# Lead-in of a fused lightning-attention and FFN kernel: decay by pow on GpSimd, copies and scalings moved between engines, matmuls on constants

## The chip, the cores and the metric

The kernel runs on one core of one Trainium2 chip. The metric is the device time of one execution in microseconds (us). Every kernel was run with a profile and then timed in rounds that alternate with runs of the kernel before on the same chip. Each run is labelled fast or slow; for a program on one core, slow means over 1.5% above the fastest run of the same kernel. All comparisons below are between fast runs. The engines are named as in the profile: PE (matmul), PEld (its weight loads), DVE (vector), ACT (scalar), POOL (GpSimd), SP (issues most of the transfers). Lnnn is a line of that kernel, so line numbers shift by a few from kernel to kernel.

## The reference, cut to what matters

```python
def _attn_ref(q, k, v, lam):                 # q, k, v: (4, 8, 768, 64); lam: (8,), 0.97 to 0.99
    block = 64
    Dmask = np.where(rel >= 0, lam[:, None, None] ** rel, 0.0)     # rel = i - j
    ...
    for b in range(nb):
        intra = (q_b k_b^T * Dmask) v_b
        inter = (q_b * lam^(pos+1)) kv_state
        out[b] = intra + inter
        kv_state = lam^block * kv_state + (k_b * lam^(block-1-pos))^T v_b

def _moe_ref(x, w_in, w_out):                # x: (3072, 512), w_in: (512, 2048), w_out: (2048, 512)
    h = x @ w_in
    g = h * np.cos(h)
    return g @ w_out
```

All decay can be put on the inputs: with q scaled by lam^pos and v by lam^-pos, the scores only need a 0/1 mask, and the state is a plain running sum. The position is counted from the middle of the sequence, so the powers run from lam^-384 to lam^383. There are 24 blocks of 128 tokens, six for each of the four sequences.

## The kernel before: the parts that the change touches

The decay factors are two tiles of 128 x 48 (48 = 6 blocks x 8 heads). ACT makes them out of Ln and Exp:

```python
nc.sync.dma_start(out=lam_bc, in_=...)                        # lam on all 128 partitions
nc.gpsimd.iota(pos, pattern=[[P, NB]], base=-S // 2, channel_multiplier=1, ...)
...
lnl = consts.tile([P, H], F32)
nc.scalar.activation(lnl, lam_bc, AF.Ln)
expo = consts.tile([P, NB, H], F32)
nc.vector.tensor_mul(expo, pos (broadcast), lnl (broadcast))
q_scale = consts.tile([P, NB, H], F32)
nc.scalar.activation(q_scale, expo, AF.Exp)
v_scale = consts.tile([P, NB, H], F32)
nc.scalar.activation(v_scale, expo, AF.Exp, scale=-1.0)
warm = consts.tile([P, 1], F32)
nc.scalar.activation(warm, halfpi, AF.Sin)                    # loads the table of the FFN's cosine
```

The work of one block of attention, as small tasks. A planner outside the chip simulates them with the durations given and emits every engine's instructions in the planned order; on the chip each engine runs its list strictly in that order. `early` is true for blocks 0 to 3, which the first FFN unit needs:

```python
early = n < TILES[0]                                          # TILES = [4, 2, 4, 4, 4, 4, 2]

def prep_q():                                                 # q_s = q * q_scale, bf16
    eng = nc.vector if early else nc.gpsimd
    eng.tensor_mul(t, live.pop(("q_f", n)), q_scale[:, c, :]...)
def prep_k():                                                 # k_b, bf16: ACT if early, else GpSimd
def prep_v():                                                 # v_pad = v * v_scale, always GpSimd, two halves
    for i in range(2):
        nc.gpsimd.tensor_mul(v_pad[n % NV][:, i::2, ...], src[:, i::2, :], v_scale[:, c, i::2]...)

def transposes():                                             # 4 of q, 4 of k, into one PSUM bank
    t = bank("ps_t", [P, 2, NP, P], BF16)
    ...
def transposes_out():                                         # one copy of both, on DVE
    nc.vector.tensor_copy(t, live.pop(("t", n)))
def transposes_bd():                                          # q_bd: q block-diagonal, two copies on DVE
...
def update_out():                                             # kv_bd: the state out of PSUM, on DVE
    for i in range(2):
        h = slice(i * D, (i + 1) * D)
        nc.vector.tensor_copy(kv_bd[n % NK][h, :, h], kv_ps[h, :, h])
```

After that come, per block, the scores (PE), the masking s_m (DVE), the values (PE) and their copy into xT (ACT). When xT holds four blocks, the FFN's first unit starts: 16 groups of 4 hidden matmuls, cosine on ACT, gating on DVE, then the projection. The two weights of 2 MB each are issued by GpSimd in four quarters each, and the load of block 4 by SP once the third quarter of the second weight has landed:

```python
ORDER = "b0 b1 b2 b3 i0 i1 i2 i3 o0 o1 o2 o3"                 # b = load of a block, i / o = quarter of w_in / w_out
...
deps = [kept[-2]] if at and (names[at - 1][0] == "b") != (which == "b") else []
```

## Time and profile before

| | before |
|---|---|
| median of four fast runs | 237.86 us (237.16 to 238.0) |
| profiled span | 236.8 us |
| copy of the values of blocks 0, 1, 2, 3 into xT starts at | 13.05, 16.39, 21.27, 25.69 |
| first weight issued / first hidden matmul | 17.21 / 26.32 |
| load of block 4 issued / first projection | 39.02 / 42.81 |

The prediction below shows the lines that this rests on. Two more lines of the kernel before are from its timeline; the columns are start in us, length in us, engine, line, operation, output<-inputs, shapes, number of instructions, and in brackets how long the engine sat idle before and what released it:

```profile
5.52 0.69 DVE L234 TENSOR_TENSOR q_s<-q_f,q_scale 128x512 bf16<-128x512 f32 x1 [1.25 <-ACT q_scale L152]
7.47 1.19 POOL L249 TENSOR_TENSOR v_pad<-v_f,v_scale 128x256 bf16<-128x256 f32 x2 [5.40 <-DMA v_f<-in_v_dram]
```

The first q is scaled at 5.52, as soon as ACT has made q_scale. The first v is scaled at 7.47 and waits for its load, not for v_scale: GpSimd is idle for 5.40 us before it.

### The profile page before, as it was taken

To read this page: it belongs to the slowest core of one execution; us is meant where nothing else is said; L and a number is where in the kernel's file an instruction comes from. 1 tells how busy PE (TensorE), PEld (TensorE's weight loads), DVE (VectorE), ACT (ScalarE), POOL (GpSimd) and SP (SyncE) were. 2 spreads that over 40 slices of the span, in tenths; PEclk is the share of its full clock that TensorE was granted. 3 is DMA by queue.
4 is the path that set the end of the run, shared out by engine and by line. 5 is a ranking of instruction groups with operands and counts; after the bars stand their busy time and mean duration, and the time that the engine had idled before them with its cause. 6 is when DMAs were issued, how large, how long until landed. Compare 5 with 4: busy or idle time off the path is not lost.

```text
span 236.8 us, 3931 instructions
## 1 busy us (share of the span) xinstructions
PE 215.4 (91%) x1447; PEld 123.9 (52%) x1472; DVE 152.8 (65%) x285; ACT 103.7 (44%) x171; POOL 68.6 (29%) x105
## 2 busy tenths in 40 slices
PE   0566799899999999999999999999999999999993
PEld 0455344456677655455555555555555545465641
DVE  5699367376999998986855776685674563433210
ACT  5330277312345446454454444435445345544420
POOL 2339100577767626342242333322000000000000
PEclk9996599999999999999999999999999999999998
DMA  6998999999999999993735110110110111111112
GB/s 125 218 189 142 206 193 197 232 221 214 249 231 233 238 226 244 204 247 64 181 77 136 55 44 0 48 44 1 47 44 4 40 47 44 44 47 44 44 44 89
DMA packets 82722, 29.61 MB, mean 125 GB/s; under 512 B 75536, under 2 KB 79632, under 8 KB 82704
## 3 DMA queue, kind: packets, MB, share of 16 engines
q1 hardware_dynamic: 78480, 25.18, 48.7%
q0 software_dynamic: 4224, 4.19, 10.9%
q8 instruction: 11, 0.18, 0.3%
q14 instruction: 7, 0.06, 0.1%
HBM read 27.27 MB, written 6.29 MB: 142 GB/s over the span
## 4 chain that ended last, share of the span: by engine, by line
PE 77%; DVE 16%; ACT 3%; issue 1%; DMA 1%
PE ps_h L362 30%; PE ps_f L400 30%; DVE q_bd L276 5%; PE ps_o L331 4%; PE ps_t L264 4%; PE ps_s L289 3%; DVE qkT L269 3%; DVE s_m L296 3%; DVE g L375 2%; PE ps_f L362 2%; DVE kv_bd L315 2%; PE ps_o L328 2%; PE ps_s L400 1%; DMA lam_bc<-in_lam_dram 1%; DVE q_s L234 1%
## 5 line engine op out<-in xcount | busy, mean ns | idle before, releaser
L369 ACT ACTIVATE cos<-ps_h,halfpi 128x512 f32<-128x512 f32 (+1 forms) x107 | 66.3, 624 | 75.8 <-PE ps_h L362 73.6
L375 DVE TENSOR_TENSOR g<-ps_h,cos 128x512 bf16<-128x512 f32 (+1 forms) x107 | 64.5, 610 | 51.5 <-ACT cos L369 50.3
L362 PE MATMUL ps_h<-xT,w_in_sb 128*128 128x512 bf16 (+1 forms) x413 | 92.8, 350 | 2.3 <-ACT xT L340 0.7
L400 PE MATMUL ps_f<-w_out_sb,g 128*128 128x512 bf16 x358 | 91.1, 379 | 1.4 <-DVE g L375 0.6
L362 PEld LDWEIGHTS <-w_in_sb 128*128 128x128 bf16 x448 | 43.4, 99 | 38.9 <-issue 4.4
L400 PEld LDWEIGHTS <-g 128*128 128x128 bf16 x384 | 36.4, 98 | 34.7 <-issue 1.3
L249 POOL TENSOR_TENSOR v_pad<-v_f,v_scale 128x256 bf16<-128x256 f32 x48 | 28.8, 621 | 55.1 <-PE ps_o L331 38.9
L296 DVE TENSOR_TENSOR s_m<-ps_s,mask 128x512 bf16<-128x512 f32 x48 | 31.3, 683 | 1.7 <-PE ps_s L289 1.4
L234 POOL TENSOR_TENSOR q_s<-q_f,q_scale 128x512 bf16<-128x512 f32 x20 | 20.9, 1046 | 29.3 <-DMA q_f<-in_q_dram 20.1
L340 ACT CAST xT<-ps_o 128x512 bf16<-128x512 f32 x24 | 14.0, 584 | 28.8 <-PE ps_o L331 28.8
L269 DVE COPY qkT<-ps_t 128x1024 bf16<-128x1024 bf16 x24 | 16.5, 689 | 15.0 <-PE ps_t L264 14.9
L331 PE MATMUL ps_o<-s_m,v_pad 128*128 128x128 bf16 x192 | 20.7, 230 | 1.0 <-DVE s_m L296 0.9
L413 ACT COPY o_sb<-ps_f 128x512 f32<-128x512 f32 x23 | 13.5, 586 | 17.5 <-PE ps_f L400 17.5
L276 DVE COPY q_bd<-qkT 64x512 bf16<-64x512 bf16 x48 | 19.8, 413 | 0.7
L289 PE MATMUL ps_s<-q_bd,qkT 128*128 128x256 bf16 x96 | 16.3, 285 | 4.4 <-DVE q_bd L276 4.3
L331 PEld LDWEIGHTS <-v_pad 128*128 128x128 bf16 x192 | 15.8, 103 | 4.6 <-issue 1.5
L315 DVE CAST kv_bd<-ps_kv 64x256 bf16<-64x256 f32 x40 | 16.8, 419 | 1.5 <-PE ps_kv L309 1.0
L264 PE MATMUL ps_t<-ident,q_s 128*128 128x128 bf16 x96 | 9.8, 227 | 6.8 <-DVE q_s L234 6.7
L328 PE MATMUL ps_o<-qkT,kv_bd 128*128 128x128 bf16 x80 | 15.7, 227 | 0.0
L289 PEld LDWEIGHTS <-qkT 128*128 128x128 bf16 x96 | 8.8, 100 | 12.9 <-DVE q_bd L276 7.6
L243 POOL CAST k_b<-k_f 128x512 bf16<-128x512 f32 x20 | 12.3, 615 | 7.1 <-issue 5.6
L264 PEld LDWEIGHTS <-q_s 128*128 128x128 bf16 x96 | 7.2, 101 | 10.3 <-DVE q_s L234 7.3
(35 smaller groups left out, 77.0 us busy)
## 6 DMA issues: line engine op xcount, KB each, us to landing
q_f<-in_q_dram SPq DMA_DIRECT2D x24, 256.0 KB, 4.9
k_f<-in_k_dram SPq DMA_DIRECT2D x24, 256.0 KB, 5.0
v_f<-in_v_dram SPq DMA_DIRECT2D x24, 256.0 KB, 4.7
out_dram<-o_sb SPq DMA_DIRECT2D x24, 256.0 KB, 2.0
w_in_sb<-in_moe_w_in_dram POOLq DMA_DIRECT2D x4, 512.0 KB, 8.4
w_out_sb<-in_moe_w_out_dram POOLq DMA_DIRECT2D x4, 512.0 KB, 14.8
lam_bc<-in_lam_dram SPq DMA_DIRECT2D x1, 4.0 KB, 2.9
```

Source lines behind the costliest of these rows:

```text
L234: eng.tensor_mul(t, live.pop(("q_f", n)), q_scale[:, c, :].unsqueeze(2).to_broadcast([P, H, D]))
L249: nc.gpsimd.tensor_mul(v_pad[n % NV][:, i::2, i * D:(i + 1) * D], src[:, i::2, :], v_scale[:, c, i::2].unsqueeze(2).to_broadcast([P, NP, D]))
L264: nc.tensor.transpose(t[:, i, p, :], src[:, 2 * p:2 * p + 2, :], ident)
L269: nc.vector.tensor_copy(t, live.pop(("t", n)))
L276: nc.vector.tensor_copy(q_bd[n % NQ][h, :, i, :], t[h, 0, :, :])
L289: nc.tensor.matmul(t[:, 2 * i:2 * i + 2, :], lhsT=live["qkT", n][:, 1, p, :], rhs=q_bd[n % NQ][:, p, :, :], start=True, stop=True)
L296: nc.vector.tensor_mul(live["s_m", n][:, 4 * half:4 * half + 4, :], live.pop(("s", n, half)), mask.unsqueeze(1).to_broadcast([P, 4, P]))
L331: nc.tensor.matmul(t[:, p, :], lhsT=v_pad[n % NV][:, 2 * p + i, :], rhs=live["s_m", n][:, 2 * p + i, :], start=(i == 0 and c == 0), stop=( ...
L362: ins = nc.tensor.matmul(t[:, :cols], lhsT=w_in_sb[:, kd, f * P:(f + 1) * P], rhs=live["xT", i][:, kd, :cols], start=(kd == 0), stop=(kd = ...
L369: nc.scalar.activation(c[:, :cols], live["h", i, f][:, :cols], AF.Sin, bias=halfpi)
L375: nc.vector.tensor_mul(live["g", i][:, f, :cols], live.pop(("h", i, f))[:, :cols], live.pop(("c", i, f))[:, :cols])
L400: nc.tensor.matmul(live["f", i, j], lhsT=live["g", i][:, f, j * P:(j + 1) * P], rhs=w_out_sb[:, f, :], start=(f == 0), stop=(f == KF - 1))
```

## The change

The intent is a shorter lead-in. The decay is made by two `pow` instructions on GpSimd, so ACT needs no Ln, no Exp and only one table load. DVE, which is full up to 25 us, gives the q scaling of blocks 1 to 3 to GpSimd and the copies of the state (kv_bd) of the early blocks to ACT. The transposes of q are copied out apart from those of k, so that q_bd can be made sooner. The first weight waits for block 2 and no longer for block 3. Matmuls on a constant fill PE's gaps up to the first hidden matmul, to keep its clock up. The last tile of the output is copied out by DVE and ACT, half each.

```diff
@@ decay
+    warm = consts.tile([P, 1], F32)
+    nc.scalar.activation(warm, halfpi, AF.Sin)
...
-    lnl = consts.tile([P, H], F32)
-    nc.scalar.activation(lnl, lam_bc, AF.Ln)
-    expo = consts.tile([P, NB, H], F32)
-    nc.vector.tensor_mul(expo, pos.unsqueeze(2).to_broadcast([P, NB, H]),
-                         lnl.unsqueeze(1).to_broadcast([P, NB, H]))
+    neg = consts.tile([P, NB], F32)
+    nc.gpsimd.iota(neg, pattern=[[-P, NB]], base=S // 2, channel_multiplier=-1,
+                   allow_small_or_imprecise_dtypes=True)
     q_scale = consts.tile([P, NB, H], F32)
-    nc.scalar.activation(q_scale, expo, AF.Exp)
     v_scale = consts.tile([P, NB, H], F32)
-    nc.scalar.activation(v_scale, expo, AF.Exp, scale=-1.0)
-    warm = consts.tile([P, 1], F32)
-    nc.scalar.activation(warm, halfpi, AF.Sin)
+    for t, e in ((q_scale, pos), (v_scale, neg)):
+        nc.gpsimd.tensor_tensor(out=t, in0=lam_bc.unsqueeze(1).to_broadcast([P, NB, H]),
+                                in1=e.unsqueeze(2).to_broadcast([P, NB, H]), op=ALU.pow)
@@ q scaling
-            eng = nc.vector if early else nc.gpsimd
+            eng = nc.vector if n == 0 else nc.gpsimd
@@ transposes
+        Tq = pl.add("PE", MM(P, 4), [a], lambda: transposes(0), pa(-0.05), get="ps_t")
+        T[n] = pl.add("PE", MM(P, 4), [b, Tq], lambda: transposes(1), pa(0.0))
+        if early:
+            Toq = pl.add("DVE", 0.42, [Tq], lambda: transposes_out(slice(0, 1)), pa(-0.02), get="qkT")
+            To[n] = pl.add("DVE", 0.42, [T[n], Toq], lambda: transposes_out(slice(1, 2)), pa(0.0))
+            first_out = Toq
+        else:
+            To[n] = first_out = pl.add("DVE", 0.7, [T[n]], lambda: transposes_out(slice(0, 2)), pa(0.0), get="qkT")
+        Tq.frees = [To[n]]
+        Tb[n] = pl.add("DVE", 0.6, [first_out, Sc.get((n - NQ, 1))], transposes_bd, pa(-0.01 if early else 0.1))
@@ state copies
+                    if early:
+                        nc.scalar.copy(kv_bd[n % NK][h, :, h], kv_ps[h, :, h])
+                    else:
+                        nc.vector.tensor_copy(kv_bd[n % NK][h, :, h], kv_ps[h, :, h])
@@ last tile
+                parts = [("DVE", "SP", slice(0, DM // 2)), ("ACT", "ACT", slice(DM // 2, DM))]
@@ release of the weights
-        deps = [kept[-2]] if at and (names[at - 1][0] == "b") != (which == "b") else []
+        deps = [kept[-4 if which != "b" else -2]] if at and (names[at - 1][0] == "b") != (which == "b") else []
@@ idle matmuls
+    def keep_awake(us, at, cols):
+        for _ in range(int(us / (cols / (1200.0 if at < 5.0 else 2400.0) + 0.0025))):
+            nc.tensor.matmul(idle_ps[:, :cols], lhsT=ident, rhs=ident[:, :cols], start=True, stop=True)
... (planner bookkeeping for the split tasks left out)
```

## The prediction

> **What bounds the kernel now.** I read the page's forty slices first, then the table of engines by windows, then the timeline of the first 50 us, and last the answers on the waits of the tensor engine and on the tile of the second weight. The slices:
>
> ```profile
> PE   0566799899999999999999999999999999999993
> ...
> DVE  5699367376999998986855776685674563433210
> ...
> PEclk9996599999999999999999999999999999999998
> DMA  6998999999999999993735110110110111111112
> ```
>
> The matrix engine (PE) is full from the fifth slice to the end, so a microsecond is won only where PE starts late or waits: the lead-in. One slice is 5.9 us. The clock dips in slices 4 and 5. DMA dips once, in slice 3, and is then full to about 105 us. The windows (columns: window and its length, then busy us of PE, weight loads, DVE, ACT, POOL, then clock, DMA share, GB/s):
>
> ```profile
> 15.00:20.00 5.00, 2.96 (x38) 2.11 (x35) 4.88 (x10) 1.20 (x2) 3.58 (x6) 0.99 0.66 101
> 20.00:25.00 5.00, 3.66 (x27) 2.73 (x27) 4.70 (x10) 0.59 (x1) 4.79 (x7) 0.50 1.24 207
> 25.00:30.00 5.00, 4.10 (x15) 1.77 (x14) 0.69 (x1) 1.34 (x3) 0.00 (x0) 0.50 1.24 204
> ...
> 100.00:200.00 100.00, 99.04 (x644) 54.09 (x655) 64.81 (x117) 46.64 (x73) 20.98 (x30) 1.00 0.26 68
> ```
>
> Until 25 us DVE is full (4.7 to 4.9 of 5) and sets the pace of the four blocks of attention that the first FFN unit needs; ACT is nearly free. From 100 us PE is 99% busy. The timeline (start, length, instruction) shows the fence posts:
>
> ```profile
> 14.61 1.19 POOL L249 TENSOR_TENSOR v_pad<-v_f,v_scale 128x256 bf16<-128x256 f32 x2 [2.38 <-DMA v_f<-in_v_dram]
> 17.21 1.68 POOL L213 DMA_DIRECT2D w_in_sb<-in_moe_w_in_dram  x2 [1.41 <-DMA k_f<-in_k_dram]
> 18.90 1.40 POOL L249 TENSOR_TENSOR v_pad<-v_f,v_scale 128x256 bf16<-128x256 f32 x2
> ...
> 21.78 3.00 POOL L216 DMA_DIRECT2D w_out_sb<-in_moe_w_out_dram  x4
> ```
> ```profile
> 25.69 0.59 ACT L340 CAST xT<-ps_o 128x512 bf16<-128x512 f32 x1 [3.83 <-PE ps_o L331]
> 26.32 0.59 PE L362 MATMUL ps_h<-xT,w_in_sb 128*128 128x512 bf16 x1 [0.67 <-ACT xT L340]
> ...
> 39.02 0.37 SPq L198 DMA_DIRECT2D q_f<-in_q_dram  x1
> ...
> 42.81 3.61 PE L400 MATMUL ps_f<-w_out_sb,g 128*128 128x512 bf16 x16 [0.64 <-DVE g L375]
> ```
>
> The FFN starts at 26.3, its first projection at 42.8. The tile view of the second weight ends with its time from issue to landing:
>
> ```profile
> DMA to landing us min/median/max: 12.0/14.8/17.4
> ```
>
> Its four issues run from 21.78 to 24.0, so its last quarter lands at 24.0 + 17.4 = 41.4. The projection at 42.8 finds it there with 1.4 us to spare, while its fourth group of four matmuls needs it only at 42.81 + 3 x 0.865 = 45.4. So the weight stream has 4.0 us of slack, and this number decides my prediction.
>
> **What the Trainium skill says.** "TensorE: Matmul & The Clock Gate", Part 1: the array runs at half clock until a window of about 3.4 us was busy, and falls back after an idle one. The trace agrees: 0.50 from about 19.9 to 29.9, matmul spacing 0.43 us at 27 to 29 and 0.216 us after 30. "ScalarE: Activation LUTs", What ACT_TABLE_LOAD costs, gives about 1283 ns for a load; the trace has three of 1.28 us, two of them behind the decay's Ln and Exp. "GPSIMD Engine Reference", section 3, puts elementwise work with two inputs at about twice DVE's time; the trace has q scaling at 1.046 us on GpSimd against 0.69 on DVE (1.5 times). It has no time for pow, nor has the trace. "DMA: Bandwidth & Descriptors", Issuing engines are not separate DMA queues: transfers share the same 16 engines whoever issues them. The trace agrees in so far as weights and block loads both run at 200 to 220 GB/s, never at their sum.
>
> **The change part by part.**
>
> Decay by pow: takes Ln, Exp and two of three table loads off ACT. Now q_scale is ready at 5.5 and ACT copies the first k at 7.04, straight after the last table load. lam lands at 3.7; with a pow of 48 elements at 1 to 2 us (a guess, ten times a multiply) q_scale comes at 4.8 to 5.8, v_scale at 6 to 8. Gain for block 0: under 1 us, none on the path, since blocks 1 to 3 are paced by their loads (v lands at 7.45, 11.05, 14.6: 3.57 us a block).
>
> DVE's work per block now: q_s 0.69, qkT 0.69, q_bd 0.6 to 0.85, s_m 1.28, kv_bd 0.85, sum 4.1 to 4.4, over the 3.57 of the loads; the backlog grows to the 24.86 at which s_m of block 3 ends. Moved away: q_s of blocks 1 to 3 (0.69 + 0.69 + 0.98 = 2.4) and kv_bd (4 x 0.85 = 3.4). Added: the copy in two halves, 2 x 0.42 for 0.69 (estimate: 0.42 is what DVE takes for half a 0.69 us tile in the gating), 4 x 0.15 = 0.6. Net 5.2 us off DVE; 2.6 to 3.3 per block, under the loads. ACT takes k_b 0.62, kv_bd about 0.8, xT 0.59 = 2.0 of 3.57. POOL takes q_s 1.05 and v_pad 1.19 = 2.24 of 3.57. The lead-in becomes load-bound.
>
> Block 3 then: k lands about 16.9; ACT is through with kv_bd of block 2 and has k_b at 17.9; transposes 18.4, second half copy 18.9, scores 19.5, s_m 20.8, values 21.3, xT 22.0. Against 26.3: 4.3 us earlier.
>
> Release of the first weight by block 2: it may go at 14.6 instead of 17.2. But POOL issues in order. By the planner's rule (of two tasks ready at once attention goes first) v_pad of block 2 (14.61 to 15.8) and the new q_s of block 3 (q lands about 15.7; to 16.9) stand ahead. So the issue comes at about 16.95, 0.25 us earlier and not 2.6. First quarter: the smallest time to landing of this tile is 5.5 us, so 22.45. FFN start about 22.5, 3.8 us earlier.
>
> Idle matmuls: PE is warm at 22.5, so the sixteen hidden groups take 16 x 0.865 = 13.8 us, to 36.35; now they take from 26.3 to 42.2, 15.9. That is 2.0 us more, 5.8 in all at this place. With the wait of 0.64 for gating the projection starts at 37.0.
>
> But its fourth group needs the last quarter of the second weight. All eight quarters move with the first: 41.4 - 0.25 = 41.15. The group is ready to run at 37.0 + 2.6 = 39.6 and waits 1.55. It starts at 41.15 where it started at 45.4: lead 4.25. Then PE waits for the evacuation (0.59 and two hand-overs, about 1.0); before, transposes of block 4 filled 0.6 to 0.8 of that gap. Block 4's load moves only by the 0.25 (its SP issue at 39.02 waits for the third quarter), its k is ready at 44.7, so the transposes come after half of the next projection. Lead left: about 3.5. Blocks 6 and 7 have their k ready 3.2 to 3.5 us before PE transposes them now (52.06 against 55.55, 56.37 against 59.55), so this lead just fits; I take off 0.1 for new small waits: 3.4. After 80 us loads run ahead and PE is the bound, so the lead stays.
>
> Tail: the last tile's evacuation by DVE and ACT halves, 0.4 for 0.59, two stores that share the same engines: 0.15. Sum: 3.4 + 0.15 = 3.55; 237.8 - 3.55 = 234.25.
>
> **Rivals.** (a) The whole 5.8 us arrives, 232.0. For it: PE is full after the lead-in. Against: the 41.4 of the weight stream and block 4's load at 39.0. It needs the first weight issued at about 15 or 15.8, which the order on POOL speaks against. (b) pow is slow. GpSimd is in order; two pows of up to 3.4 us each are caught up by block 3 (it has 1.3 us free per block and 3.7 before the first v). At 5 us each the weight would be issued some 3 us late, and all loads with it: gain about zero, 237 to 238; beyond, slower. Nothing in the profile measures pow. (c) GpSimd and DVE hinder each other in the lead-in: q_bd is 0.59 a pair alone and 0.85 beside GpSimd's weight issue at 17.4, q_s 0.98 in place of 0.69. The FFN then starts at 24; 1.5 us of wait for the weight absorbs that, and the total stays near 234.5. (d) Idle matmuls hold real ones up: at half clock they take 0.11 us instead of 0.058 and the planned 60% of a gap becomes 115%. That costs some tenths per block before the clock rises, also absorbed: 234.5. (e) The static order of all later work is planned anew, worth plus or minus 0.8.
>
> **Range and chances.** Most errors of the lead-in are swallowed by the wait for the weight; the upside is capped by it. Centre 234.2, range 232.8 to 235.9. Faster by over 2% means under 233.05: 0.17, mostly rival (a). Slower by over 2% needs a slow pow: 0.03. Within 2%: 0.80.
>
> **What would show it.** Right: DVE in the window of 15 to 20 well under 4.5 us busy; clock 1.0 from about 10 us on; first hidden matmul at 22 to 23; first weight issue within 0.6 us of 17; PE waiting 1 to 2 us at 39 to 41 inside the first projection; SP's load of block 4 at 38.5 to 39; PE ahead by 3 to 4 us at 100 us. Wrong: a weight issue before 16 or after 18, a pow over 3.4 us, no wait in the first projection, or a lead that has shrunk under 2 us by 100 us because DVE, 95% busy from 60 to 100, cannot follow.

## The result, and the profile after

The changed kernel is slower: 246.73 us median of four fast runs (246.13 to 247.31) against 237.86. The ratio is 1.0379, with a 95% interval of 1.0346 to 1.0412. (A ratio here is the mean time of one kernel's fast runs over that of the other's fast runs of the same rounds, so it is not quite the ratio of the two medians.) The profiled span went from 236.8 to 244.4 us.

| | before | after |
|---|---|---|
| xT copies of blocks 0, 1, 2, 3 start at | 13.05, 16.39, 21.27, 25.69 | 23.13, 27.77, 31.84, 35.27 |
| first weight issued | 17.21 | 26.38 |
| first hidden matmul | 26.32 | 35.91 |
| load of block 4 issued | 39.02 | 48.56 |
| first projection | 42.81 | 50.52 |

These are the forty slices of the changed kernel (6.1 us each; busy tenths of each engine, granted clock of PE in tenths, and the share of the transfer engines):

```profile
PE   4065799979999999999999999999999999999993
...
DVE  4051756735799999898668457756847373342310
...
POOL 6999950027776864532340432232000000000000
PEclk9997999999999999999999999999999999999999
DMA  6990499999999999999546201101100111011112
```

POOL reads 9 in slices 2 to 5, while DVE reads 0, 5, 1 and 7. DMA stands still in slice 4: the first four blocks have landed, and the weights have not been asked for. PE is at 0 in the second slice and reads 9 from the sixth (from 30.5 us) on, with one 7 where the first projection begins; in the kernel before it read 9 from the sixth slice of 5.9 us too (with one 8), but had no empty one behind the first. The windows show the same in figures (window and its length, then busy us of PE, weight loads, DVE, ACT and POOL with their instruction counts, granted clock, share of the transfer engines, GB/s):

```profile
5.00:10.00 5.00, 0.00 (x0) 0.00 (x0) 0.00 (x0) 0.62 (x1) 5.00 (x1) 1.00 1.32 223
...
20.00:25.00 5.00, 3.84 (x40) 3.54 (x39) 1.40 (x4) 1.94 (x4) 5.00 (x8) 0.66 0.01 3
...
100.00:200.00 100.00, 100.00 (x671) 55.03 (x669) 68.52 (x125) 47.10 (x73) 23.70 (x34) 1.00 0.36 87
```

From 5 to 10 us one single POOL instruction fills the whole window, and PE and DVE do nothing at all. From 20 to 25 us transfers run at 3 GB/s. From 100 us PE has no gap (99.04 of 100 us before, with some records missing there). So the time was lost in the lead-in and not won back. The timeline names the instruction:

```profile
3.74 8.05 POOL L155 TENSOR_TENSOR q_scale<-lam_bc,pos 128x48 f32<-128x48 f32 x1 [1.55 <-DMA lam_bc<-in_lam_dram]
11.77 8.00 POOL L155 TENSOR_TENSOR v_scale<-lam_bc,neg 128x48 f32<-128x48 f32 x1
19.84 1.19 POOL L249 TENSOR_TENSOR v_pad<-v_f,v_scale 128x256 bf16<-128x256 f32 x2
...
26.38 0.98 POOL L213 DMA_DIRECT2D w_in_sb<-in_moe_w_in_dram  x1
```

One pow of 48 elements per partition takes 8 us. Two of them hold GpSimd until 19.77, and everything in its queue stands behind them: the first v at 19.84 in place of 7.47, the q of blocks 1 to 3, and last the first weight. The line of v_pad has no bracket any more: its input has long been there, and GpSimd comes to it without a pause. The waits of the first 36 us say the same from the other side (who waited for whom: us in total, times, longest):

```profile
DVE q_s L234 <- POOL q_scale L155: 7.6, 1, 7.6
PE ps_kv L315 <- POOL v_pad L249: 4.6, 1, 4.6
```

DVE waits 7.6 us for the first pow, and PE another 4.6 us for the first v behind the second. The fence posts of the prediction now stand here (timeline; the count in the PE line ends with the window asked for):

```profile
35.27 0.59 ACT L349 CAST xT<-ps_o 128x512 bf16<-128x512 f32 x1 [0.23 <-PE ps_o L340]
35.91 1.45 PE L371 MATMUL ps_h<-xT,w_in_sb 128*128 128x512 bf16 x6
...
48.56 0.37 SPq L198 DMA_DIRECT2D q_f<-in_q_dram  x1
```

The hidden matmuls start when the xT copy of block 3 ends (35.27 + 0.59 = 35.86). The first weight quarter was issued at 26.38, and the shortest time to landing of a quarter in this trace is 5.5 us, so it was there at about 32 (an estimate from these two numbers). It is the attention of the first four blocks, not the weight, that set the start.

At the end of the kernel, the split of the last copy can be read off the timelines. Before, and then after:

```profile
232.85 0.59 ACT L413 COPY o_sb<-ps_s 128x512 f32<-128x512 f32 x1 [2.00 <-PE ps_s L400]
```
```profile
240.53 0.42 DVE L422 COPY o_sb<-ps_s 128x256 f32<-128x256 f32 x1 [5.92 <-DMA out_dram<-o_sb]
240.99 0.37 ACT L422 COPY o_sb<-ps_s 128x256 f32<-128x256 f32 x1 [2.46 <-DVE o_sb L422]
```

The halves did not run side by side. ACT's half starts when DVE's is done (240.53 + 0.42 = 240.95) and is shown as released by it, so it waits for a semaphore of DVE's; no run tried it without this wait. From the start of the copy to the end of the span it is 236.8 - 232.85 = 3.95 us before and 244.4 - 240.53 = 3.87 after, so 0.08 us was won.

### The profile page after: what moved, and what is told of

It reads as the page before. It is cut to its first block, busy times and chain, and to the rows that moved or that the text cites. A ratio compares the mean times of both kernels' runs of the same rounds, so it can differ in the third digit from the quotient of the medians.

```text
span 244.4 us, 4231 instructions
## 1 busy us (share of the span) xinstructions
PE 221.6 (91%) x1608; PEld 131.3 (54%) x1608; DVE 147.4 (60%) x278; ACT 103.6 (42%) x174; POOL 88.0 (36%) x111
## 4 chain that ended last, share of the span: by engine, by line
PE 76%; DVE 11%; POOL 5%; issue 3%; DMA 2%; ACT 2%; POOLq 0%
PE ps_f L409 31%; PE ps_h L371 29%; PE ps_o L340 4%; DVE q_bd L276 3%; PE ps_s L295 3%; PE ps_t L265 3%; POOL v_scale L155 3%; DVE g L384 3%; DVE qkT L270 2%; DVE s_m L302 2%; PE ps_f L371 2%; PE ps_kv L315 2%; POOL q_scale L155 1%; PE ps_o L337 1%; DMA lam_bc<-in_lam_dram 1%
## 5 line engine op out<-in xcount | busy, mean ns | idle before, releaser
L409 PE MATMUL ps_f<-w_out_sb,g 128*128 128x512 bf16 x368 | 92.6, 379 | 1.3 <-ACT o_sb L422 0.7
L234 POOL TENSOR_TENSOR q_s<-q_f,q_scale 128x512 bf16<-128x512 f32 x23 | 24.2, 1051 | 23.7 <-DMA q_f<-in_q_dram 19.7
L270 DVE COPY qkT<-ps_t 128x1024 bf16<-128x1024 bf16 (+1 forms) x28 | 17.2, 614 | 22.5 <-PE ps_t L265 22.1
L422 ACT COPY o_sb<-ps_f 128x512 f32<-128x512 f32 x23 | 13.5, 586 | 21.7 <-PE ps_f L409 21.7
L340 PE MATMUL ps_o<-s_m,v_pad 128*128 128x128 bf16 x192 | 20.0, 223 | 0.4 <-DVE s_m L302 0.4
L349 ACT CAST xT<-ps_o 128x512 bf16<-128x512 f32 x24 | 14.0, 585 | 12.5 <-PE ps_o L340 12.4
L276 DVE COPY q_bd<-qkT 64x512 bf16<-64x512 bf16 x48 | 18.7, 390 | 0.7
L295 PE MATMUL ps_s<-q_bd,qkT 128*128 128x256 bf16 x96 | 15.6, 279 | 1.9 <-DVE qkT L270 1.6
L340 PEld LDWEIGHTS <-v_pad 128*128 128x128 bf16 x192 | 15.1, 100 | 3.7 <-issue 0.7
L324 DVE CAST kv_bd<-ps_kv 64x256 bf16<-64x256 f32 x32 | 13.4, 419 | 1.2 <-PE ps_kv L315 1.0
L467 PE MATMUL ps_h<-ident 128*128 128x128 bf16 (+1 forms) x136 | 12.1, 245 | 1.6 <-POOL ident masks.py:199 1.6
```

Of the source, the lines that this page charges most:

```text
L234: eng.tensor_mul(t, live.pop(("q_f", n)), q_scale[:, c, :].unsqueeze(2).to_broadcast([P, H, D]))
L270: nc.vector.tensor_copy(live["qkT", n][:, sides], live["t", n][:, sides])
L276: nc.vector.tensor_copy(q_bd[n % NQ][h, :, i, :], t[h, 0, :, :])
L295: nc.tensor.matmul(t[:, 2 * i:2 * i + 2, :], lhsT=live["qkT", n][:, 1, p, :], rhs=q_bd[n % NQ][:, p, :, :], start=True, stop=True)
L340: nc.tensor.matmul(t[:, p, :], lhsT=v_pad[n % NV][:, 2 * p + i, :], rhs=live["s_m", n][:, 2 * p + i, :], start=(i == 0 and c == 0), stop=( ...
L409: nc.tensor.matmul(live["f", i, j], lhsT=live["g", i][:, f, j * P:(j + 1) * P], rhs=w_out_sb[:, f, :], start=(f == 0), stop=(f == KF - 1))
```

## The experiments

Two theories were tested first. **Theory A:** pow alone is to blame, through GpSimd's queue, and the rest of the change is worth something. **Rival B:** the lead-in would have caught up with a late start, and other parts of the change (GpSimd's new q scaling, the new order, the idle matmuls) carry a large share of the loss. Twelve kernels were run, in three calls of four, each call on another chip. All gave correct results. The kernel before had medians of 237.86 (runs 1 to 4), 238.33 (5 to 8) and 237.64 (9 to 12).

### 1. The changed kernel with the decay made as before

```diff
-    neg = ...iota...
-    for t, e in ((q_scale, pos), (v_scale, neg)):
-        nc.gpsimd.tensor_tensor(out=t, ..., op=ALU.pow)
+    nc.scalar.activation(lnl, lam_bc, AF.Ln)
+    nc.vector.tensor_mul(expo, pos ..., lnl ...)
+    nc.scalar.activation(q_scale, expo, AF.Exp)
+    nc.scalar.activation(v_scale, expo, AF.Exp, scale=-1.0)
```

> The changed kernel with the decay worked out as before (Ln, Exp and their table loads on ACT), all other parts kept. Theory A: the two pows of 8.0 us each on GpSimd, an engine in order, delay v_pad, q_s and the issue of the first weight, and are the whole of the loss; the rest of the change works as predicted. Then: first weight issue at about 17 us, FFN start 22 to 23.5, wait of 1 to 2 us in the first projection, time 233 to 235.5. Rival B: another part (q scaling on GpSimd, idle matmuls in PE's queue, ACT copies) loses too. Then the time is 236 or more. Rival C: the whole 5.8 us of the earlier start arrives: 232.

Measured: 236.46 us (235.63 to 237.93), ratio to before 0.9938 (0.9892 to 0.9984). Taking pow out, and nothing else, won back 246.73 - 236.46 = 10.3 us. The first hidden matmul came at 24.98, 10.9 us earlier than with pow. So the loss is pow's, and the rest of the change is worth about 1.4 us (0.4 to 2.6 by the interval of the ratio). That is less than the 3.55 predicted for it, and the time fell on the rival's side of the expectation (236 or more): the other parts lose nothing, but they gain far less than theory A had them gain. Two lines of its timeline show one reason, to which experiments 5 to 7 come back:

```profile
16.80 1.04 POOL L235 TENSOR_TENSOR q_s<-q_f,q_scale 128x512 bf16<-128x512 f32 x1 [0.94 <-DMA q_f<-in_q_dram]
17.78 1.68 POOL L214 DMA_DIRECT2D w_in_sb<-in_moe_w_in_dram  x2
```

The weight was released by block 2, but its issue stands behind the q scaling of block 3 in GpSimd's queue, and that waited 0.94 us for its load. It left at 17.78, later than the 17.21 of the kernel before.

### 2. The kernel before with pow, and nothing else

(The table load for the cosine moves ahead with it, since Ln and Exp are gone.)

```diff
-    (Ln, multiply, Exp, Exp)
+    for t, e in ((q_scale, pos), (v_scale, neg)):
+        nc.gpsimd.tensor_tensor(out=t, ..., op=ALU.pow)
```

> The kernel before with only the decay by pow on GpSimd (and the Sin table load moved ahead). Theory A: q_scale at 11.8, v_scale at 19.8, three v_pads, the first weight issued at 23.4 (6.2 us late), everything after it late by as much: 243 to 245. Rival B (pow is not the whole): the time comes out near 238 to 240.

Measured: 252.06 us (251.41 to 252.91), ratio 1.0598 (1.0553 to 1.0644). Pow alone costs the old kernel 14.2 us, more than was expected of it and more than it costs the changed kernel. The first v came at 19.81, as in the changed kernel, and the first hidden matmul at 38.68, 12.4 us later than before: here DVE still had all the q scalings and state copies to do in each block, which may be why. The direction confirms theory A; the size was missed, and the 1.8 us between 12.4 and 14.2 were not traced.

### 3. Experiment 1 without the matmuls on constants

```diff
-        if t.eng == "PE" and now < hid_t[0, 0].start + 1e-6:
+        if False and t.eng == "PE" and now < hid_t[0, 0].start + 1e-6:
```

> As the first run of this call, with the idle matmuls taken out too. Theory A with the prediction's step that the warm clock's 2 us are swallowed by the wait for the last quarter of the second weight: the clock is 0.5 for some windows before and after the FFN start, hidden ends up to 2 us later, yet the time is within 0.7 us of the first run. Rival: the clock pays in full, 1.5 to 2 us slower than the first run.

Measured: 236.50 us (236.19 to 238.88), ratio 0.9955 (0.9899 to 1.001), against 236.46 with them; the first hidden matmul at 25.06 against 24.98. They are worth nothing that the medians show, and cost nothing. One of the four runs without them took 238.88 us at a mean clock of 0.982 (the others 0.997); the four with them had 0.997 to 1.00. Whether they guard against such a run is open.

The clock column needs care. The traces hold no clock record before the first rise, and the column reads 1.00 there although the matmuls run at half rate: in the kernel before, four of 128 columns take 0.61 us at 6.27 (column 1.00), 0.40 at 14.72 (1.00) and 0.61 at 21.27 (0.50). By the records the clock rises at 13.08 in the kernel before, at 11.45 in experiment 1, and at 18.44 here. So the constants bring the rise 7 us forward, but the clock is up in both when the FFN starts at 25. After the rise it stays up here, for example (columns as above):

```profile
20.00:25.00 5.00, 2.83 (x35) 2.09 (x33) 3.17 (x7) 2.60 (x6) 4.21 (x6) 1.00 1.25 208
```

In the kernel before, it fell to 0.50 from 19.91 to 30.15. The traces suggest what decides this. The records between rise and fall last 6.83 and 10.24 us there and 3.41 and 3.42 in the changed kernel, all multiples of 3.41. If the traces are cut into stretches of 3.41 us counted from the first rise, the clock fell after those in which PE was busy for 0.00 us (the changed kernel), 1.42 (experiment 2), 1.53 (the profile of experiment 10) and 1.61 (the kernel before), and in none of the fourteen traces after one with 2.02 or more, up to 228 us. Here the least after the rise is 2.02. The changed kernel also shows what constants can't do: they stand in PE's list, in order, behind the matmul that waits for the first v. So PE did nothing from 16.99 to 20.40, and the clock fell from 20.40 to 23.82 in spite of them.

### 4. One pow in place of two, the other factor by a reciprocal on DVE

```diff
-    for t, e in ((q_scale, pos), (v_scale, neg)):
+    for t, e in ((q_scale, pos),):
         nc.gpsimd.tensor_tensor(..., op=ALU.pow)
+    nc.vector.reciprocal(v_scale, q_scale)
```

> The changed kernel with one pow on GpSimd in place of two; v_scale is the reciprocal of q_scale, taken on DVE. Theory A: POOL is free at 11.8 in place of 19.8; v_pad, q_s and v_pad follow without waits, the first weight is issued at about 18.5 (1.3 us later than in the kernel before), FFN start about 24, time 235 to 236.5: half the pows take off far more than half of the loss, as what is under the loads' pace is caught up. Rival (cost is in proportion to pow time): 241 to 242.

Measured: 243.92 us (242.65 to 244.8), ratio 1.024 (1.0195 to 1.0285). This was a miss, and the one that taught most. The first v came at 12.29, and by then the first two blocks had landed, with the next ones 3.57 us apart. If the lead-in were paced by its loads, it would have caught up by block 3. It did not: the first hidden matmul came at 32.14, which is 7.2 us after that of experiment 1, and the time is 7.5 us longer. The chain of what ended last, between two blocks whose data were long there, shows why (start us, us, what):

```profile
23.81 0.24 PE ps_t L266 x4
...
24.07 0.43 DVE qkT L271
...
24.53 0.28 DVE q_bd L277
...
24.83 0.43 DVE q_bd L277
...
25.29 0.43 DVE qkT L271
...
25.77 0.41 PE ps_s L296 x2
...
26.20 0.70 DVE s_m L303
...
26.94 0.27 PE ps_o L341 x2
...
27.44 0.24 PE ps_t L266 x4
```

From the q transposes of block 2 at 23.81 to those of block 3 at 27.44 there are 3.63 us with no gap of more than 0.06: transposes, copy, two q_bd copies, second copy, scores, masking, values, and only then the transposes of the next block, which PE has in its list behind the first half of the values of this one. (The lines left out are pauses of 0.05 us at most and, before the last line, 0.23 us of PE's own work, 0.06 of it on constants.) It is one serial chain through PE and DVE, about as long as the 3.57 us that a block takes to load. In these 3.63 us PE was busy for 3.22 (matmuls on constants included), DVE for 2.91, POOL for 2.81 and ACT for 1.88: no engine is full, and still nothing can be caught up.

### 5. Experiment 1 with ACT copying k of the next block ahead of the state of this one

```diff
+        if early and n - 1 in Uo:
+            Uo[n - 1].deps.append(b)
```

> As the first run (decay by Ln and Exp), with one thing changed: on ACT the copy of k of block n+1 goes ahead of the state copies of block n, for the first four blocks. In the first run ACT, in order, held k of block 3 (landed about 17) back to 20.3 behind state copies of block 2, a chain of about 4 us a block. Theory D: that order made the FFN start at 25.0 in place of the 22 of the prediction, but the time is not set there: from 50 to 105 us DVE is full and paced by when block 4 arrives. Then: FFN start 22 to 24, time within 0.7 us of the first run (235.8 to 237.0). Rival E (the FFN start sets the time): 1.5 to 2.5 us faster than the first run.

Measured: 235.99 us (235.64 to 237.87), ratio 0.991 (0.9879 to 0.9941); the first hidden matmul at 24.26 instead of 24.98. The two intervals overlap, so no gain of this order is shown. But its timeline shows the wait for the weight that the prediction counted on:

```profile
42.31 1.02 PE L412 MATMUL ps_f<-w_out_sb,g 128*128 128x512 bf16 x4 [0.69 <-DMA w_out_sb<-in_moe_w_out_dram]
```

The fourth group of the first projection waits 0.69 us for the last quarter of the second weight. It starts at 42.31; in experiment 1, 0.16 us of wait put it at 42.33. So the earlier FFN start was used up here, as the prediction said; it had put the wait at 1.55 us.

### 6. Experiment 1 with the state copies on ACT for all blocks

```diff
-                    if early:
+                    if True:
                         nc.scalar.copy(kv_bd[n % NK][h, :, h], kv_ps[h, :, h])
...
-            Uo[n] = pl.add("ACT" if early else "DVE", 0.85, ...)
+            Uo[n] = pl.add("ACT", 0.85, ...)
```

> As the first run, with the state copies on ACT for all blocks, not the first four alone: takes 0.85 us a block off DVE after 45 us (17 copies pairs in all, about 9 of them between 50 and 105 us). Theory D (DVE sets the pace from 50 to 105 us and eats the lead): the evacuation of block 13 comes 2 us or more earlier than in the first run (101.9) and the time falls by 1 to 2.5 us, to 234 to 235.5. Rival (PE or the block loads set the pace there): within 0.5 us of the first run.

Measured: 234.61 us (234.45 to 234.68), ratio 0.9833 (0.9814 to 0.9851), 1.85 us under experiment 1. The lead-in is the same (first hidden matmul 24.89), so the gain is made later: the xT copy of block 13 starts at 100.14 in place of 101.93 (1.8 us earlier; 2 or more was expected). (The kernel before ran at slightly different medians; by the ratios to it, the gain is 2.5 us.) The window of 60 to 80 us, for experiment 1 and then for this one (columns as above):

```profile
60.00:80.00 20.00, 19.06 (x194) 14.68 (x193) 19.39 (x43) 9.28 (x19) 14.64 (x21) 1.00 1.21 236
```
```profile
60.00:80.00 20.00, 19.94 (x206) 15.51 (x204) 18.34 (x38) 12.69 (x30) 14.18 (x21) 1.00 1.16 237
```

DVE (third busy figure) is busy for 19.39 of 20 us in experiment 1, and for 19.40 in the kernel before: 97%. PE has about 1 us of gaps there. With the state copies on ACT, DVE falls to 18.34, and PE has 19.94 of 20. So in this stretch DVE probably held PE back, and a lead from the lead-in ran up against it. Two things keep this from being shown. DVE's share alone does not decide it: in experiment 12 DVE is busy for 19.15 of these 20 us, and PE has no gap all the same. And the planner puts all later work in a new order when a task changes its engine (rival (e) of the prediction), which no run separates.

### 7. Experiment 1 with q of block 3 scaled on DVE

```diff
-            eng = nc.vector if n == 0 else nc.gpsimd
+            eng = nc.vector if n in (0, 3) else nc.gpsimd
```

> As the first run, with q scaling of block 3 on DVE again, so that nothing stands between v_pad of block 2 and the first weight's issue on GpSimd: issue at about 15.9 in place of 17.8, weights fill the DMA pause of 17 to 19, loads of block 4 start at 37.8 to 38.5 in place of 39.8. Theory D: block 4's attention comes 1 to 1.5 us earlier and the time falls by 0.5 to 1.5, to 235 to 236. Rival (weights only take bandwidth from blocks 2 and 3 of the lead-in, nothing won): 236.3 or more.

Measured: 234.51 us (234.12 to 235.69), ratio 0.9833 (0.981 to 0.9856), 1.95 us under experiment 1, a larger gain than expected (235 to 236). With the q scaling of block 3 out of GpSimd's queue, the weight goes as soon as block 2 allows it, at 15.73 in place of 17.78, and the load of block 4 with it, at 37.75 in place of 39.79 (timeline):

```profile
15.73 2.44 POOL L214 DMA_DIRECT2D w_in_sb<-in_moe_w_in_dram  x3
```

The first hidden matmul moved by only 0.34 us (24.64), the load of block 4 by 2.04 us, and the time by 1.95 (2.5 by the ratios). That the loads of block 4 and those after it bind here is what these three numbers suggest; the runs do not separate it from the shorter wait for the second weight, which moves with it.

### 8. Experiments 4 and 5 together

```diff
+    nc.vector.reciprocal(v_scale, q_scale)        # one pow only
...
+        if early and n - 1 in Uo:
+            Uo[n - 1].deps.append(b)               # k ahead of the state on ACT
```

> The kernel with one pow and a reciprocal (243.9 measured), with the copy of k of block n+1 ahead of the state copies of block n on ACT. Theory D: the late start of block 0 (q_s at 12.1 in place of 5.5) was not caught up since each block followed the last in a serial chain of about 4 us; with k ahead the chain opens, the FFN starts at 29 to 30 in place of 32.1, and the time falls by 2 to 3 us, to 241 to 242. Rival (GpSimd itself is the chain there): within 0.7 us of 243.9.

Measured: 244.03 us (243.4 to 245.39), ratio 1.0236 (1.0206 to 1.0266), and the first hidden matmul at 32.26 against 32.14 in experiment 4. The theory behind it, that ACT's order stretched the chain of experiment 4, falls. The chain runs through PE's order and DVE.

### 9. Pow for 8 elements only, twice; the rest by multiplication

Block 0's factor and the step lam^128 by pow, the other five blocks by multiplying with the step on GpSimd, v_scale by reciprocals on DVE:

```diff
+    nc.gpsimd.tensor_tensor(out=q_scale[:, 0, :], in0=lam_bc, in1=pos[:, 0:1].to_broadcast([P, H]), op=ALU.pow)
+    nc.gpsimd.tensor_tensor(out=step, in0=lam_bc, in1=c128, op=ALU.pow)
+    nc.vector.reciprocal(v_scale[:, 0, :], q_scale[:, 0, :])
+    for c in range(1, NB):
+        nc.gpsimd.tensor_mul(q_scale[:, c, :], q_scale[:, c - 1, :], step)
```

> The changed kernel with pow kept on GpSimd, but for 8 elements a partition twice (the first block's scale, and lam to the 128th) in place of 48 twice; the other blocks' scales by five multiplications, v's by reciprocals on DVE. If pow's time is in proportion to its elements (8.04 us for 48, so 0.167 us each), each pow takes 1.3 to 1.5 us, the first q scaling comes at 5.3 to 6.5 and the time is that of the run with Ln and Exp, 235.5 to 237.5. If it is a fixed cost, each takes 8 us and the time stays at 244 or more.

Measured: 239.59 us (238.41 to 240.23), ratio 1.0063 (1.002 to 1.0107), a miss by 2 us. The time of pow itself is what this run was made for:

```profile
3.68 1.68 POOL L154 TENSOR_TENSOR q_scale<-lam_bc,pos 128x8 f32<-128x8 f32 x1 [1.60 <-DMA lam_bc<-in_lam_dram]
5.34 1.63 POOL L155 TENSOR_TENSOR step<-lam_bc,c 128x8 f32<-128x8 f32 x1
7.05 1.33 POOL L158 TENSOR_TENSOR q_scale<-q_scale,step 128x8 f32<-128x8 f32 x5
```

Eight elements take 1.68 us and forty-eight 8.05. The slope is (8.05 - 1.68) / 40 = 0.159 us per element of a partition, with 1.68 - 8 x 0.159 = 0.41 us left over. So pow's cost grows with the elements and is no fixed start-up; that it is a straight line, two sizes can't show. The miss has the cause of experiment 4 again, on a small scale. The reciprocal for the later blocks waits on DVE for the last multiply and stands ahead of the first transposed copy (qkT), which starts at 8.74, against 6.87 in experiment 1. These 1.9 us and a little more became 3.0 us at the first hidden matmul (28.02) and 3.1 us in the time. The weight, by contrast, left at 16.81, 1 us *earlier* than in experiment 1. So it is the attention chain that sets the start of the FFN here, not the weight.

### 10. The kernel before with the state copies of all blocks on ACT

```diff
-                    nc.vector.tensor_copy(kv_bd[n % NK][h, :, h], kv_ps[h, :, h])
+                    nc.scalar.copy(kv_bd[n % NK][h, :, h], kv_ps[h, :, h])
```

> The kernel before with one thing changed: the state copies on ACT for all blocks. Theory D (DVE is the pace both to 25 us and from 50 to 105): 0.85 us a block off DVE in both stretches, time 234.5 to 236.5. Rival (the weight stream and block loads set both): 237.5 or more.

Measured: one fast run at 234.23 us, and five that were labelled slow at 237.85 to 238.95, the profiled one with a mean granted clock of 0.978. One fast run gives no interval. The labels rest on time alone here: the four other slow runs had a clock of 0.999 to 1.00, no lower than the 0.998 of the fast one, so the fast one may as well be the exception. Whether this single move gives the old kernel most of what is to be had stays open.

### 11. Experiments 1, 5, 6 and 7 together

```diff
+            eng = nc.vector if n in (0, 3) else nc.gpsimd         # 7
+            Uo[n - 1].deps.append(b)                              # 5
+            Uo[n] = pl.add("ACT", 0.85, ...)                      # 6
```

> The run with Ln and Exp, with all three mends together: k ahead on ACT, q of block 3 on DVE so that the weights go out first, state copies on ACT for all blocks. The second and third alone gave 234.6 and 234.5. If the two act on different stretches (load of block 4 earlier; DVE faster after it), they add in part: 232.3 to 233.9. If they remove the same wait: 234.2 to 234.8.

Measured: 234.11 us (233.31 to 234.38), ratio 0.983 (0.9796 to 0.9865). That is between the two ranges expected and decides for neither.

### 12. Experiments 1, 6 and 7 together

```diff
+            eng = nc.vector if n in (0, 3) else nc.gpsimd         # 7
+            Uo[n] = pl.add("ACT", 0.85, ...)                      # 6
```

> As the run with all three mends, without k ahead on ACT. Theory D says the order on ACT is not on the path: within 0.5 us of it. Rival: 0.7 us or more slower.

Measured: 233.21 us (232.31 to 234.2), ratio 0.9798 (0.9762 to 0.9834). This is the best of all and beats both kernels: 4.4 us under the kernel before in the same rounds, 13.5 us under the changed one. The order of experiment 5, which experiment 11 has in addition, does not help: 0.9 us more at the median (within 0.5 was expected), with overlapping ranges. The gains of 6 and 7 over experiment 1 (1.85 and 1.95) come to 3.25 us together (2.5, 2.5 and 3.3 by the ratios), so they may overlap in part. Here PE is busy for 19.93 of the 20 us between 60 and 80, and DVE for 19.15.

### The delay of block 0, followed to the end

Start of the xT copy of each early block, first hidden matmul, and median time:

| kernel | xT 0 | xT 1 | xT 2 | xT 3 | FFN | time |
|---|---|---|---|---|---|---|
| before | 13.05 | 16.39 | 21.27 | 25.69 | 26.32 | 237.86 |
| after | 23.13 | 27.77 | 31.84 | 35.27 | 35.91 | 246.73 |
| 1, no pow | 12.28 | 16.52 | 20.92 | 24.34 | 24.98 | 236.46 |
| 4, one pow | 19.54 | 24.49 | 28.17 | 31.50 | 32.14 | 243.92 |
| 9, pow of 8 | 14.70 | 19.84 | 23.84 | 27.38 | 28.02 | 239.59 |

Against experiment 1, block 0 is late by 10.9, 7.3 and 2.4 us in the three kernels with pow, the FFN by 10.9, 7.2 and 3.0, and the whole by 10.3, 7.5 and 3.1. A delay of block 0 goes through to the end nearly one to one. It is not the loads of the later blocks that carry it: the load of block 4 is issued 8.8 and 1.4 us later than in experiment 1 (39.79) in the first two, and 0.8 us earlier in the third. The steps from block to block are 3.4 to 4.6 us in the changed kernel, where the loads have long landed, and 3.4 to 4.4 in experiment 1, where they land every 3.57.

## Why the prediction was wrong

**The step that failed** is in the part on the decay: "with a pow of 48 elements at 1 to 2 us (a guess, ten times a multiply) q_scale comes at 4.8 to 5.8, v_scale at 6 to 8". One pow measured 8.05 us, four to eight times the guess; q_scale came at 11.8 and v_scale at 19.8. The sum's term for pow was "under 1 us, none on the path". It measured 10.3 us on the path (experiment 1 against the changed kernel).

**The second step that failed** stood behind it and would have failed for a smaller pow too: "two pows of up to 3.4 us each are caught up by block 3 (it has 1.3 us free per block and 3.7 before the first v)". That counted busy time on single engines. On the chip the blocks hang together in one serial chain, with 3.3 to 5.1 us from block to block in experiments 4 and 9, so nothing is caught up. For the same reason "the lead-in becomes load-bound" was wrong: without pow the xT copies come 4.24, 4.40 and 3.42 us apart, against 3.57 of the loads, and the FFN starts at 24.98 where 22 to 22.5 was predicted.

**Rival (b), a slow pow, is what happened**, by the way that it describes: GpSimd in order, the weight and all loads late. It was given too small a chance (0.03), because a duration that no page and no trace gave was allowed a narrow range. Even rival (b) looked to the wrong release: it feared for the weight, while the attention chain set the start. In the changed kernel the weight lay ready some 4 us before it was used (the estimate of about 32 above, against 35.91).

**Rival (c), GpSimd and DVE in each other's way, is seen.** The pair of q_bd copies takes 0.59 us alone, and in experiment 1 up to 1.43 beside the q scaling that moved to GpSimd:

```profile
16.56 1.43 DVE L277 COPY q_bd<-qkT 64x512 bf16<-64x512 bf16 x2
```

GpSimd's q scaling runs from 16.80 to 17.84 in that trace, and this pair ends at 17.99. A single copy of them takes 0.28 us at the shortest and up to 1.13. The Trainium skill, "SBUF — State Buffer", section "Who interferes with whom", describes this: a DVE copy in one of its two-port modes and a GpSimd instruction need the same port pair, which one of them holds for its whole instruction while the other blocks. The trace agrees in the duration; it does not show the port. The prediction had this wait absorbed by the wait for the weight. It lies on the serial chain to the FFN's start, and there, in experiment 1, the wait for the weight did absorb it: the fourth group of the first projection still had 0.16 us to wait.

**What held.** The weight's issue stuck behind the q scaling of block 3: predicted 16.95, measured 17.78 and 16.84 (experiments 1 and 3), and 15.73 once that was moved (experiment 7); the mechanism held, though the 0.8 us more in experiment 1 count below. The hidden groups at full clock took 24.98 to 38.95, 14.0 us against 13.8 predicted; 38.95 is the projection's start at 39.59 less its wait of 0.64. The wait for the last quarter of the second weight exists, but is smaller: 0.69 us in experiment 5, and in experiment 1 the sixteen matmuls took 3.77 in place of 3.61, so 0.16, in place of 1.55. ACT's copy of the first k came earlier (6.04, 7.04 before) and won nothing, as said. The tail won 0.08, not 0.15.

**Without pow, the prediction would still have been too low:** 236.46 measured, 234.25 predicted. The range ended at 235.9, which the interval of the ratio (235.3 to 237.5 us) takes in, while the centre lies outside it. Of the missing 2.2 us, 1.2 are there at the fourth group of the first projection. It was predicted at 41.15 and starts at 42.33 in experiment 1: ready at 42.17 after the late FFN start, and held 0.16 more by the weight, which was issued 0.8 us later than predicted. The kernel before starts it at 45.40, so the lead is 3.07 and not 4.25.

The rest went later: by the medians the lead is 1.4 at the end, where 3.55 with the tail was predicted. So "the lead stays" was wrong too. How it went is less clear. The order of the later work was planned anew, so single marks compare different amounts of work: the copy of the third output tile leads by 4.35 us (55.40, before at 59.75), but the values of block 4 by 0.5 (51.15 against 51.66), those of block 9 by 0.3 (75.45 against 75.77) and those of block 13 by 0.4 (101.93 against 102.34). DVE at 97% in between was the prediction's own last way to be wrong, and the load of block 4 came at 39.79 and not by 39. Experiments 6 and 7, each of which takes away one of the two, give 1.85 and 1.95 us back.

**The idle matmuls** were counted at 2.0 us of the FFN's start-up. The full clock came, but without them too (experiment 3), so in these traces they earned none of this gain. The kernel before lost the clock after a stretch in which PE was busy for 1.61 of 3.41 us; with the rest of the change and no pow (experiments 1 and 3) no stretch after the rise is below 2.02.

## What to carry to other kernels

An operation whose duration is in no trace and on no page has to be timed alone before it goes onto an in-order queue that also carries transfers; an error of a factor of four to eight there outweighs every careful sum beside it. A delay at the head of a statically ordered chain of blocks is not caught up because every single engine has time to spare: add up one block's chain from hand-over to hand-over, and if that is as long as the pace of the loads, the delay goes through to the end. And a lead won early is kept only where no other engine is full later: look at the busy shares of the stretch behind it (DVE at 97% here) before it is counted. A high share is a warning and not yet a proof: with DVE at 96%, experiment 12 had no gap on PE.

## What the Trainium skill lacked or had wrong

- "GPSIMD Engine Reference" has no duration for pow, and its factor of about two against DVE for two-input elementwise work (section 3) does not extend to it. The runs show 8.05 us for 48 elements per partition and 1.68 us for 8, so about 0.16 us an element and 0.41 us beside it. A multiply of 512 elements took 1.04 us on the same engine, and one of 8 elements 0.27 us (five in 1.33).
- "TensorE: Matmul & The Clock Gate", Part 1, has the clock fall after an idle window of about 3.4 us, and does not say how much work keeps a window from counting as idle. In these traces the clock fell after stretches of 3.41 us with 0.00 to 1.61 us of PE busy, and did not after 2.02 or more.
